# 1.3 FFN half-steps in every round of attention, with each weight unit's VectorE work behind the round's maximum

## The chip, the cores and the metric

The kernel runs on one core of a Trainium2 chip. The metric is the device time of one execution in microseconds (us). Three runs of the kernel before gave 940.33, 939.21 and 939.44 us, so the median is 939.44 us.

## What is computed

Three layers follow each other on 2304 tokens (4 batches of 576, 8 heads of 64, model width 512): linear attention with random features, a gated FFN (RMS norm, SiLU gate, hidden width 1536), and a mixture of 8 experts with capacity routing. Cut to what matters:

```
proj = x @ omega.T                 # per head: 64 -> 128 features, for q and for k
phi  = exp(h - max(h)) / sqrt(m)   # h = proj - |x|^2 / 2
kv, z = phi(k).T @ v, sum(phi(k)); attn = phi(q) @ kv / (phi(q) @ z + 1e-6)
xn   = attn / rms(attn) * rms_g    # 2304 x 512
y    = (silu(xn @ w_gate) * (xn @ w_val)) @ w_out
out  = top-capacity routing of y to 8 experts, each relu(y @ w1[e]) @ w2[e]
```

The weights `w_gate`, `w_val` and `w_out` come in as 64-bit floats and are turned into 32-bit ones on the chip.

## The kernel before

**Rounds of attention.** Attention is a list of 76 items: a `KItem` takes 256 or 128 key tokens of a head pair, a `QItem` half the heads of 128 query tokens. `run_tick(tick)`, called a *round* here, runs one lag of each of up to six items: lag 0 projects (TensorE, tile `pp`, L387 to L392), takes the maximum (VectorE, `mx`, L396) and the exponential (ScalarE, `ft`, L399); lag 1 is the product with v for keys (L439, L442) or the transposes for queries (L485); lag 2 the product with kv (L491, L496) and the division; lags 3 to 5 the norm and the transposes into the FFN's input blocks `xh`, `xl` (L501, L549, L550).

**Half-steps of the FFN.** An input block is 512 tokens (four of them, and a last one of 256). A *half-step* `(j, f, v)` is 12 matmuls of block `j`, 128 hidden columns `f`, gate (`v = 0`) or value (`v = 1`), into one PSUM tile `gv` (`ffn_pe`, L642 to L645). `gv` has two buffers (pool `psG`). `ffn_el` empties it: for the gate a tanh on ScalarE (L654) and a product on VectorE (L655), for the value a product on VectorE (L663 for block 0, L667 for the others). `ffn_step_pe` and `ffn_step_el` run the next half-step that is ready. There are 120 half-steps; the first block is ready at round 23, and the last rounds leave over 40 to a loop behind attention.

**Weight units.** The 36 units convert the 64-bit weights: 24 `WgvUnit` (gate and value, two for each `f`) and 12 `WoUnit`. A unit lives four lags: lag 0 a magnitude on ScalarE (L570), lag 1 `word()`, three VectorE operations (L574, L575, L576), lag 2 for a `WgvUnit` a cast on ScalarE (L598) and a difference on GpSimd (L599). A `WoUnit` has TensorE work too: at lag 2 four transposes into a `gv` tile (L613), emptied by ScalarE (L627), at lag 3 matmuls into the same tile (L617), emptied by two small VectorE operations into `wog` (L629, L630). So it holds one of the two `gv` buffers from its transposes until those. `conv_pe(pace)` adds `pace` to a due count and starts a unit for each whole one; `conv_el` runs the units' other operations and starts the load of a later one. Half-step `(0, f, v)` needs the two units of `f`.

**What sets the order.** TensorE's instructions stand in the order in which the code writes them. On the other engines a scheduler orders them at build time, by priority and by its own estimate of when each can run; attention's part has a raised priority. Every engine, and SP's queue of transfers, then runs its list strictly in that order. In a round the code writes: `conv_pe`, attention's TensorE part, a half-step, attention's other part, `conv_el`, loads, `ffn_step_el`. From round 23 on, as long as gate and value units are left, an extra pass adds one more unit and one more half-step (`SUB = 1`), so that such a round has two units and two half-steps; after that one half-step a round and half a unit. When a new input block needs a buffer that is taken (rounds 60 and 78), the rest of the old block is run off at once.

Of the kernel before, what the change touches and what calls it, by code (L numbers as in the profile page):

```python
# [14 lines left out]
OP = mybir.AluOpType  # L15
AX = mybir.AxisListType
# [18 lines left out]
KF = FF // 128  # L35
# [11 lines left out]
EARLY = 6  # L47
LOADS = 9
SKIP = 2
SUB = 1  # L50
PACE = (0.5, 1.0, 0.5)
FFN_AT = 23
AHEAD_A = 200
HB = 6
# [236 lines left out]
def kernel(ctx, tc, qT, kT, kC, v1, vC, om, wgv, rms, wo, wg2, w1, w2, cfd, trd, cid, out, dbg=None):  # L291
    nc = tc.nc
# [35 lines left out]
    st = {}  # L328
# [64 lines left out]

    def feat(pp, n, ng):
        mx = at.tile([128, 4], F32, name="mx")
        nc.vector.tensor_reduce(out=mx[:n, :ng], in_=pp[:n, :ng], axis=AX.X, op=OP.max, negate=True)  # L396
        ft = at.tile([128, 4, M], F32, name="ft")
        for g in range(ng):
            nc.scalar.activation(ft[:n, g], pp[:n, g], AF.Exp, bias=mx[:n, g:g + 1])  # L399
        return ft  # L400

    class KItem:
# [42 lines left out]
        def el(self, lag):  # L445
            b, p, g = self.b, self.p, self.g
            if lag == 0:
                self.ft = feat(self.pp, 128, 2 * len(self.ts))
            elif lag == 1 and g == 2:
                r, w = p // 2, b // 2  # L450
                if w not in kvs:
                    kvs[w] = at.tile([128, H, 2, D + 1], F32, name="kvs", bufs=1)
                nc.scalar.copy(kvs[w][:, 4 * r:4 * r + 4, b % 2, :].rearrange("p (o h) d -> p h o d", o=2),
                               st.pop(("pk", b, r))[:, :4 * (D + 1)].rearrange("p (h o d) -> p h o d", h=2, o=2))
# [123 lines left out]
    class WgvUnit(Unit):  # L578
# [9 lines left out]
        def el(self, lag):  # L588
            f, s_ = self.f, slice(self.g * 512, (self.g + 1) * 512)
            if lag == 0:  # L590
                self.magnitude(fp.tile([128, DM], F32, name="dw", bufs=DW))
            elif lag == 1:
                self.word()
            elif lag == 2:
                if self.g == 0:
                    wsl[f] = wpool.tile([128, 2, 1024], F32R, name="wc")
                w = wsl[f]
                nc.scalar.copy(w[:, 0, s_], self.t)  # L598
                nc.gpsimd.tensor_sub(w[:, 1, s_], self.t, w[:, 0, s_])  # L599
                gvs.add((f, self.g))  # L600

    class WoUnit(Unit):
# [16 lines left out]
        def el(self, lag):  # L619
            f = self.f  # L620
            if lag == 0:
                self.magnitude(fp.tile([128, DM], F32, name="dw", bufs=DW))
            elif lag == 1:
                self.word()
                nc.sync.dma_start(wo_dr[f], self.t)
            elif lag == 2:
                nc.scalar.copy(self.t, self.pt.rearrange("p k m -> p (k m)"))  # L627
            elif lag == 3:
                nc.vector.tensor_copy(wog[:, f, 0, :], self.pw)  # L629
                nc.vector.tensor_sub(wog[:, f, 1, :], self.pw, wog[:, f, 0, :])  # L630
                wogs.add(f)
# [16 lines left out]
    def ffn_el(j, f, v, pg):  # L648
        n = WIDTH[j]
        nh = n // HB2  # L650
        if v == 0:
            fst["th"] = fp.tile([128, BLK], F32, name="th")
            th = fst["th"][:, :n]
            nc.scalar.activation(th, pg, AF.Tanh, scale=0.5)  # L654
            nc.vector.scalar_tensor_tensor(th, th, 1.0, pg, op0=OP.add, op1=OP.mult)  # L655
            return
        th = fst["th"][:, :n]
        hp = fp.tile([128, BLK // HB2, 2, HB2], F32R, name="hp")
        hf = hp.bitcast(F32)
        dst = h_dr[nh * j:nh * j + nh] if nh > 1 else h_dr[NT // HB2 - 1:]  # L660
        dst = dst[:, :, f].rearrange("b p x -> p b x")
        if j == 0:
            nc.vector.scalar_tensor_tensor(hf[:, :, 0], pg.rearrange("p (b t) -> p b t", b=nh), 0.5,  # L663
                                           th.rearrange("p (b t) -> p b t", b=nh), op0=OP.mult, op1=OP.mult)
            nc.sync.dma_start(dst[:, :, :HB2], hf[:, :, 0])
            return
        nc.vector.scalar_tensor_tensor(th, pg, 0.5, th, op0=OP.mult, op1=OP.mult)  # L667
        h = th.rearrange("p (b t) -> p b t", b=nh)
        nc.scalar.copy(hp[:, :nh, 0], h)  # L669
        nc.gpsimd.tensor_sub(hp[:, :nh, 1], h, hp[:, :nh, 0])  # L670
        nc.sync.dma_start(dst, hf[:, :nh].rearrange("p b l t -> p b (l t)"))
        fq.append((j, f, hp))
# [30 lines left out]
    def ffn_rank_el():  # L703
        for c0 in rks:
            ranks(nc, st["eng"], fp, cf[:, C_T:C_N].rearrange("p (a b) -> p a b", b=E), L, R, c0, 2)
        rks.clear()

    def ffn_step_pe():
        if not ready or ready[0][1:] not in gvs or (fq and fq[0][1] not in wogs):
            return False  # L710
        j, f, v = ready.pop(0)
        pg = ffn_pe(j, f, v)
        if (f, v) == (KF - 1, 1):
            del xblk[j]
        ffn_rank()
        if v and fq:
            ffn_lg(*fq.pop(0))
        fst["el"] = (j, f, v, pg)
        return True

    def ffn_step_el():
        if "el" in fst:
            j, f, v, pg = fst.pop("el")
            ffn_el(j, f, v, pg)
            ffn_rank_el()
            return j, f, v
        return None
# [43 lines left out]
            nc.tensor.matmul(sink, idle[:, :128], idle[:, 128:], start=True, stop=True)  # L771

    NLAG = 6
    conv = dict(live=[], due=0.0, next=0, load=3)

    def conv_pe(pace):
        conv["due"] += pace
        conv["live"] = [(lag + 1, u) for lag, u in conv["live"] if lag < 3]
        while conv["due"] >= 1 and conv["next"] < len(useq):
            conv["due"] -= 1  # L780
            conv["live"].append((0, useq[conv["next"]]))
            conv["next"] += 1
        for lag, u in conv["live"]:
            u.pe(lag)

    def conv_el():
        for lag, u in conv["live"]:
            u.el(lag)
            if lag == 1 and conv["load"] < len(useq):
                useq[conv["load"]].load()  # L790
                conv["load"] += 1

    def run_tick(tick):
        live = [(lag, items[tick - lag]) for lag in range(NLAG) if 0 <= tick - lag < len(items)]
        conv_pe(PACE[0] if tick < FFN_AT else PACE[1] if conv["next"] < 2 * KF else PACE[2])
        with tc.high_priority(offset=AHEAD_A):
            for lag, it in live:
                it.pe(lag)
        ffn_step_pe()
        for lag, it in live:  # L800
            if lag == 5 and isinstance(it, QItem) and it.hf and it.c * 128 // BLK not in xblk:
                while len(xblk) > 1:
                    ffn_step_el()
                    if not ffn_step_pe():
                        conv_el()
                        conv_pe(1)
        with tc.high_priority(offset=AHEAD_A):
            for lag, it in live:
                it.el(lag)
            if tick + 1 < len(items):  # L810
                items[tick + 1].split()
        conv_el()
        if tick + AHEAD < len(items):
            items[tick + AHEAD].load()
        ffn_step_el()
        if tick >= FFN_AT and conv["next"] < 2 * KF:
            for r in range(SUB):
                conv_pe(1)
                ffn_step_pe()
                conv_el()  # L820
                ffn_step_el()

    with tc.manual_schedule(engines={mybir.EngineType.PE}):
        warm(10)
        for tick in range(len(items) + NLAG - 1):
            run_tick(tick)
            if tick < 2:
                warm(4)
# [41 lines left out]
    lates, step = [], 0  # L870
# [327 lines left out]
```

## Time and profile before

| | us |
|---|---|
| median of three runs | 939.44 |
| the profiled execution's own time | 941.22 |
| its span (first to last instruction) | 939.4 |
| TensorE busy in the span | 912.3 (97%) |
| VectorE, ScalarE, GpSimd busy | 536.6, 372.5, 220.8 |

The profiled execution took 1.8 us more than the median; 1.8 us of its own time lies around the span. The trace has, for each instruction, its engine, line, tile, start and duration, and for idle time what ended it. TensorE's matmuls overlap, so that a matmul's duration is longer than the distance to the next; time is therefore best read from one start to another. "PEclk" is the clock that TensorE was granted, as a share of 2.4 GHz.

### The profile page before, as it was taken

What the parts mean: (1) busy time and instruction counts of PE and PEld (TensorE: products, weight loads), DVE (VectorE), ACT (ScalarE), POOL (GpSimd) and SP (SyncE); (2) the same over time, 40 slices, a digit from 0 to 9 for tenths busy, and PEclk for the clock granted to TensorE, in tenths of its full rate; (3) what the DMA queues carried; (4) which work ended last, traced back from release to release, by engine and by line L of the source; (5) the groups of instructions that cost most, each with busy time, mean ns of one, the idle gap of its engine ahead of it and who ended that gap; (6) DMA issues with size and microseconds to landing.
All of it is one profiled execution on the core that took longest, in us unless ns stands there. A gap on an engine that the chain in (4) does not pass through costs nothing.

```text
span 939.4 us, 16221 instructions
## 1 busy us (share of the span) xinstructions
PE 912.3 (97%) x6219; PEld 792.0 (84%) x6219; DVE 536.6 (57%) x1230; ACT 372.5 (40%) x843; POOL 220.8 (24%) x294
## 2 busy tenths in 40 slices
PE   8998889999999999999999999999999999999996
PEld 7887679888888888777789777777779999999996
DVE  3799976655542455341255566666664655566651
ACT  5975445554553445233233110010014444455441
POOL 1345421122232332254323000000011222121211
PEclk9998989999999999999999999999999999999998
DMA  8546653354222121158665477767632666666650
GB/s 289 178 155 211 212 169 117 124 189 163 68 71 92 61 90 46 70 211 288 205 202 201 148 210 210 207 198 211 183 93 90 181 202 192 201 194 187 186 170 26
DMA packets 111486, 152.61 MB, mean 162 GB/s; under 512 B 6448, under 2 KB 70576, under 8 KB 111408
## 3 DMA queue, kind: packets, MB, share of 16 engines
q1 hardware_dynamic: 105600, 137.28, 46.8%
q0 software_dynamic: 3072, 9.44, 3.3%
q10 hardware_dynamic: 2736, 4.85, 1.4%
q8 instruction: 49, 0.80, 0.4%
q14 instruction: 29, 0.24, 0.1%
HBM read 107.50 MB, written 44.04 MB: 161 GB/s over the span
## 4 chain that ended last, share of the span: by engine, by line
PE 75%; issue 6%; DVE 2%; POOL 2%; DMA 1%; ACT 0%; SPq 0%; POOLq 0%; ACTq 0%; DVEq 0%
PE py L953 15%; PE gv L642 9%; PE gv L643 9%; PE gv L645 9%; PE ph L1067 3%; PE ph L1064 3%; PE ph L1065 3%; PE py L1075 3%; PE py L1076 3%; PE py L1077 3%; PE pm L496 2%; PE cnt L180 2%; PE pm L439 1%; PE pp L387 1%; PE pm L485 1%
## 5 line engine op out<-in xcount | busy, mean ns | idle before, releaser
L642 PE MATMUL gv<-xh,wc 128*128 128x512 f32 (+1 forms) x480 | 182.1, 386 | 8.0 <-DVE th L655 8.0
L643 PE MATMUL gv<-xh,wc 128*128 128x512 f32 (+1 forms) x480 | 176.4, 374 | 0.0
L953 PE MATMUL py<-wc,ht 128*128 128x512 f32 x648 | 167.3, 404 | 0.0
L953 PEld LDWEIGHTS py<-wc,ht 128*128 128x128 f32 x648 | 114.8, 189 | 19.0
L645 PE MATMUL gv<-xl,wc 128*128 128x512 f32 (+1 forms) x480 | 120.0, 372 | 0.0
L642 PEld LDWEIGHTS gv<-xh,wc 128*128 128x128 f32 x480 | 91.9, 191 | 27.5 <-DVE th L655 9.4
L643 PEld LDWEIGHTS gv<-xh,wc 128*128 128x128 f32 x480 | 91.9, 191 | 14.4
L645 PEld LDWEIGHTS gv<-xl,wc 128*128 128x128 f32 x480 | 86.5, 191 | 16.1
L655 DVE SCALAR_TENSOR_TENSOR th<-th,gv 128x512 f32<-128x512 f32 (+1 forms) x60 | 37.9, 631 | 103.8 <-ACT th L654 103.7
L399 ACT ACTIVATE ft<-pp,mx 128x128 f32<-128x128 f32 x288 | 82.8, 373 | 26.1 <-DVE mx L396 23.4
L924 DVE TENSOR_TENSOR wc<-ws,wc 128x512 fp32r<-128x512 f32 x128 | 84.7, 682 | 0.0
L670 POOL TENSOR_TENSOR hp<-th,hp 128x512 fp32r<-128x512 f32 (+1 forms) x48 | 58.7, 1222 | 107.5 <-ACT hp L669 101.5
L1075 PE MATMUL py<-ehh,wc 128*128 128x288 f32 x256 | 77.7, 304 | 0.0
L1076 PE MATMUL py<-ehl,wc 128*128 128x288 f32 x256 | 75.9, 297 | 0.0
L1077 PE MATMUL py<-ehh,wc 128*128 128x288 f32 x256 | 75.8, 296 | 0.0
L1064 PE MATMUL ph<-exh,wc 128*128 128x288 f32 x256 | 71.6, 302 | 0.0
L1065 PE MATMUL ph<-exh,wc 128*128 128x288 f32 x256 | 69.8, 295 | 0.0
L934 ACT CAST wc<-ws 128x1024 fp32r<-128x1024 f32 x64 | 66.9, 1046 | 2.4 <-ACT ys L964 2.4
L964 ACT COPY ys<-py 128x512 f32<-128x512 f32 x18 | 10.6, 588 | 144.2 <-PE py L953 103.3
L654 ACT ACTIVATE th<-gv 128x512 f32<-128x512 f32 (+1 forms) x60 | 33.2, 554 | 65.5 <-PE gv L645 60.0
L396 DVE TENSOR_REDUCE mx<-pp 128x4 f32<-128x512 f32 (+1 forms) x76 | 49.8, 656 | 15.9 <-PE pp L392 8.4
L669 ACT CAST hp<-th 128x512 fp32r<-128x512 f32 (+1 forms) x48 | 27.1, 565 | 77.7 <-DVE th L667 77.6
(217 smaller groups left out, 1709.7 us busy)
## 6 DMA issues: line engine op xcount, KB each, us to landing
ws<-in_w_dram SPq DMA_DIRECT2D x64, 512.0 KB, 4.4
ht<-h_dr SPq DMA_DIRECT2D x54, 512.0 KB, 4.2
h_dr<-hp SPq DMA_DIRECT2D x36, 512.0 KB, 2.8
ws<-in_wgv_dram SPq DMA_DIRECT2D x24, 512.0 KB, 4.1
h_dr<-hp SPq DMA_DIRECT2D x24, 256.0 KB, 2.3
ws<-in_wo_dram SPq DMA_DIRECT2D x12, 512.0 KB, 3.8
h_dr<-ht SPq DMA_DIRECT2D x12, 512.0 KB, 3.6
y_dr<-ys ACTq DMA_DIRECT2D x18, 256.0 KB, 4.3
```

What stands on the lines that cost most here:

```text
L399: nc.scalar.activation(ft[:n, g], pp[:n, g], AF.Exp, bias=mx[:n, g:g + 1])
L642: nc.tensor.matmul(pg[:, :n], w[:, 0, v, k], xh[:, k, :n], start=(k == 0), stop=False)
L643: nc.tensor.matmul(pg[:, :n], w[:, 1, v, k], xh[:, k, :n], start=False, stop=False)
L645: nc.tensor.matmul(pg[:, :n], w[:, 0, v, k], xl[:, k, :n], start=False, stop=(k == KD - 1))
L924: nc.vector.tensor_sub(w[:, 1, h], sv[:, h], w[:, 0, h])
L934: nc.scalar.copy(w[:, 0], sv)
L953: nc.tensor.matmul(py, ht[:, i4, a], w[:, l, f % 2], start=(f == 0 and n == 0), stop=(f == KF - 1 and n == 2))
L1064: nc.tensor.matmul(ph, w[:, 0, k, m], xh[:, k], start=(k == 0), stop=False)
L1065: nc.tensor.matmul(ph, w[:, 1, k, m], xh[:, k], start=False, stop=False)
L1075: nc.tensor.matmul(py, w[:, 0, k], hh[:, k], start=(k == 0), stop=False)
L1076: nc.tensor.matmul(py, w[:, 0, k], hl[:, k], start=False, stop=False)
L1077: nc.tensor.matmul(py, w[:, 1, k], hh[:, k], start=False, stop=(k == KE - 1))
```

## The change

The extra pass goes. In its place every round from 23 on adds 0.3 to a count, and a second half-step is run whenever that count reaches one: 1.3 half-steps a round to the end of attention. The units' pace becomes 0.5, 0.9 and 0.7 a round: ahead of round 23, while gate and value units are left, and for the `WoUnit`s. A unit's `word()` is wrapped so that its VectorE operations stand behind the maximum of the same round in VectorE's list. And `ffn_step_el` is written ahead of `conv_el`.

```diff
-SUB = 1
-PACE = (0.5, 1.0, 0.5)
+STEP = 1.3
+PACE = (0.5, 0.9, 0.7)
@@ feat
-        nc.vector.tensor_reduce(out=mx[:n, :ng], in_=pp[:n, :ng], axis=AX.X, op=OP.max, negate=True)
+        st["mx"] = nc.vector.tensor_reduce(out=mx[:n, :ng], in_=pp[:n, :ng], axis=AX.X, op=OP.max, negate=True)
@@ WgvUnit.el and WoUnit.el
             elif lag == 1:
-                self.word()
+                with tc.issue_after(st["mx"].ins):
+                    self.word()
@@ run_tick
+        ffn_step_el()
         conv_el()
         if tick + AHEAD < len(items):
             items[tick + AHEAD].load()
-        ffn_step_el()
-        if tick >= FFN_AT and conv["next"] < 2 * KF:
-            for r in range(SUB):
-                conv_pe(1)
+        if tick >= FFN_AT:
+            conv["step"] += STEP - 1
+            if conv["step"] >= 1:
+                conv["step"] -= 1
                 ffn_step_pe()
-                conv_el()
                 ffn_step_el()
```

**VectorE, rounds 24 and 25.** A list of the kernel before, from one round's maximum to the next (the numbers behind the names tell tiles apart; `dw` is a unit's word, `th` and `hp` are the half-steps' results, `kh` a query tile's cast):

```order
L396 TENSOR_REDUCE mx_882<-pp_857 128x4
L576 SCALAR_TENSOR_TENSOR dw_683<-ws_472,dw_683 128x512
L574 TENSOR_SCALAR dw_757<-dw_757 128x512
L575 SCALAR_TENSOR_TENSOR dw_757<-ws_554,dw_757 128x512
L576 SCALAR_TENSOR_TENSOR dw_757<-ws_554,dw_757 128x512
L574 TENSOR_SCALAR dw_829<-dw_829 128x512
L655 SCALAR_TENSOR_TENSOR th_906<-th_906,gv_869 128x512
L575 SCALAR_TENSOR_TENSOR dw_829<-ws_645,dw_829 128x512
L576 SCALAR_TENSOR_TENSOR dw_829<-ws_645,dw_829 128x512
L663 SCALAR_TENSOR_TENSOR hp_932<-gv_909,th_906 128x2x256
L574 TENSOR_SCALAR dw_852<-dw_852 128x512
L396 TENSOR_REDUCE mx_959<-pp_935 128x4
```

The changed kernel's list from the maximum of round 27 to that of round 29 (line numbers are up to two higher there):

```order
L396 TENSOR_REDUCE mx_1018<-pp_997 128x2
L382 CAST kh_1069<-qt_931 128x256
L657 SCALAR_TENSOR_TENSOR th_994<-th_994,gv_981 128x512
L574 TENSOR_SCALAR dw_979<-dw_979 128x512
L575 SCALAR_TENSOR_TENSOR dw_979<-ws_876,dw_979 128x512
L576 SCALAR_TENSOR_TENSOR dw_979<-ws_876,dw_979 128x512
L665 SCALAR_TENSOR_TENSOR hp_1027<-gv_1005,th_994 128x2x256
L396 TENSOR_REDUCE mx_1061<-pp_1039 128x4
L382 CAST kh_1115<-qt_1037 128x256
L657 SCALAR_TENSOR_TENSOR th_1073<-th_1073,gv_1048 128x512
L396 TENSOR_REDUCE mx_1106<-pp_1081 128x4
```

Between two maxima there were eight word operations and two half-steps' results, with word operations on both sides of `th`; now there are three and two in one round and none and one in the next, and `th` stands ahead of the words.

**TensorE, a `WoUnit` and the half-steps beside it.** Before, around the second unit (`gv_1541` is the unit's tile, the other `gv` tiles are half-steps):

```order
L645 MATMUL gv_1497<-xl_548,wc_1070 128x512 x4
L613 MATMUL gv_1541<-cf_69,dw_1471 128x128 x4
...
L485 MATMUL pm_1553<-cf_69,ft_1512 128x128 x4
L496 MATMUL pm_1558<-kvs_256,qp_1517 128x65 x4
L501 MATMUL pm_1563<-cf_69,xn_1461 128x128 x4
...
L645 MATMUL gv_1568<-xl_548,wc_1070 128x512 x4
L617 MATMUL gv_1541<-wg2s_81,dw_1471 128x8 x4
```

The changed kernel, around its fifth unit (`gv_2224`) and the start of its sixth (`gv_2300`):

```order
L614 MATMUL gv_2224<-cf_69,dw_2164 128x128 x4
...
L439 MATMUL pm_2124<-vt_2037,ft_2200 128x65 x4
...
L647 MATMUL gv_2240<-xl_1482,wc_370 128x512 x4
L683 MATMUL lg_2142<-hp_2156,wog_74 16x512
L684 MATMUL lg_2142<-hp_2156,wog_74 16x512
...
L647 MATMUL gv_2280<-xl_1482,wc_501 128x512 x4
L618 MATMUL gv_2224<-wg2s_81,dw_2164 128x8 x4
L614 MATMUL gv_2300<-cf_69,dw_2220 128x128 x4
```

Before, one half-step lay between a unit's two TensorE parts, and attention's part between any two uses of a `gv` buffer. Now a second half-step (`gv_2280`) can lie there with only the two `lg` matmuls ahead of it, and the next unit's transposes can follow a unit's matmuls at once.

**ScalarE, ahead of round 23.** Before, the cast of round 23's keys (`kh_779`) stood ahead of round 21's exponentials (`ft_745`):

```order
L549 CAST xh_547<-pm_700 128x4x128
L364 CAST kh_779<-kt_728 128x256
L399 ACTIVATE ft_745<-pp_732,mx_743 128x128 x4
L364 CAST kh_822<-kt_728 128x256
L570 ACTIVATE dw_504<-ws_351 128x512
L399 ACTIVATE ft_774<-pp_759,mx_772 128x128 x2
```

Now:

```order
L549 CAST xh_547<-pm_700 128x4x128
L399 ACTIVATE ft_745<-pp_732,mx_743 128x128 x2
L399 ACTIVATE ft_774<-pp_759,mx_772 128x128
L399 ACTIVATE ft_745<-pp_732,mx_743 128x128
L399 ACTIVATE ft_774<-pp_759,mx_772 128x128
L364 CAST kh_779<-kt_728 128x256
L364 CAST kh_822<-kt_728 128x256
```

The two casts moved behind the exponentials of rounds 21 and 22, and one magnitude (`dw_504`) ahead of them.

## Rows read from the trace of the kernel before

**Rows 1.** The page: busy time of each engine, share of the span, instructions.

```profile
PE 912.3 (97%) x6219; PEld 792.0 (84%) x6219; DVE 536.6 (57%) x1230; ACT 372.5 (40%) x843; POOL 220.8 (24%) x294
```

**Rows 2.** Windows: stretch, length, busy PE, PEld, DVE, ACT, POOL, PEclk, DMA share, GB/s.

```profile
80.00:100.00 20.00, 16.63 (x76) 13.86 (x76) 19.75 (x25) 9.77 (x21) 10.72 (x8) 0.83 0.66 206
100.00:120.00 20.00, 16.05 (x84) 13.05 (x83) 19.45 (x27) 11.43 (x25) 9.69 (x8) 1.00 0.70 205
120.00:140.00 20.00, 16.68 (x86) 13.90 (x85) 14.64 (x41) 7.69 (x21) 3.82 (x6) 0.83 0.50 168
160.00:180.00 20.00, 20.00 (x143) 18.34 (x141) 13.46 (x31) 10.63 (x28) 3.38 (x6) 1.00 0.40 128
```

**Rows 3.** Waits of TensorE in 60 to 140 us: total, times, longest.

```profile
PE gv L642 <- DVE th L655: 7.1, 5, 3.4
PE pm L485 <- ACT ft L399: 2.4, 2, 2.1
PE pm L491 <- DVE x L518: 1.5, 1, 1.5
```

**Rows 4.** TensorE's timeline, rounds 23 to 26: start, us, operation, idle before.

```profile
59.01 0.50 PE L642 MATMUL gv<-xh,wc 128*128 128x512 f32 x1
64.59 0.28 PE L387 MATMUL pp<-omh,kh 128*128 128x256 f32 x1
71.75 0.28 PE L387 MATMUL pp<-omh,kh 128*128 128x256 f32 x1
...
84.43 0.79 PE L642 MATMUL gv<-xh,wc 128*128 128x512 f32 x1 [3.37 <-DVE th L655]
89.72 0.48 PE L642 MATMUL gv<-xh,wc 128*128 128x512 f32 x1
```

**Rows 5.** VectorE operations of 0 to 420 us by shape: busy us, mean ns.

```profile
L396 DVE TENSOR_REDUCE mx<-pp 128x4 f32<-128x512 f32 x68 | 46.5, 684 | 11.6 <-PE pp L392 7.5 <-PE pp L389 2.1 <-ACT wc L598 1.0
L575 DVE SCALAR_TENSOR_TENSOR dw<-ws,dw 128x512 int32<-128x512 int32 x36 | 34.0, 948 | 0.8 <-DVE dn L514 0.3
L576 DVE SCALAR_TENSOR_TENSOR dw<-ws,dw 128x512 int32<-128x512 int32 x36 | 28.8, 803 | 0.5
L655 DVE SCALAR_TENSOR_TENSOR th<-th,gv 128x512 f32<-128x512 f32 x38 | 26.0, 684 | 58.6 <-ACT th L654 58.6
L574 DVE TENSOR_SCALAR dw<-dw 128x512 int32<-128x512 int32 x36 | 23.2, 646 | 4.4 <-ACT dw L570 4.4
```

**Rows 6.** TensorE's timeline, a later round of queries without a wait.

```profile
143.62 0.37 PE L387 MATMUL pp<-omh,kh 128*128 128x256 f32 x1
146.06 0.48 PE L642 MATMUL gv<-xh,wc 128*128 128x512 f32 x1
```

**Rows 7.** Timelines of two engines: what follows a unit's matmuls and a gate's half-step.

```profile
137.48 1.05 PE L617 MATMUL gv<-wg2s,dw 128*128 128x8 f32 x8
138.39 0.36 PE L387 MATMUL pp<-omh,kh 128*128 128x256 f32 x1
...
138.64 0.17 DVE L629 CAST wog<-gv 128x8 fp32r<-128x8 f32 x1 [0.23 <-PE gv L617]
...
295.78 1.07 PE L645 MATMUL gv<-xl,wc 128*128 128x512 f32 x4
296.68 0.39 PE L642 MATMUL gv<-xh,wc 128*128 128x512 f32 x1
297.58 0.69 DVE L655 SCALAR_TENSOR_TENSOR th<-th,gv 128x512 f32<-128x512 f32 x1 [3.17 <-ACT th L654]
```

**Rows 8.** A window of 5 us, columns as in rows 2.

```profile
110.00:115.00 5.00, 3.10 (x17) 2.46 (x15) 4.93 (x6) 1.81 (x4) 3.00 (x3) 1.00 0.57 176
```

**Rows 9.** ScalarE and GpSimd operations on key tiles, 0 to 420 us, as in rows 5.

```profile
L364 ACT CAST kh<-kt 128x256 fp32r<-128x256 f32 x24 | 10.0, 417 | 3.8 <-PE pp L388 3.7
L365 POOL TENSOR_TENSOR kl<-kt,kh 128x256 fp32r<-128x256 f32 x24 | 18.0, 749 | 53.8 <-ACT kh L364 38.2 <-PE pm L485 6.9 <-PE pm L442 4.8
L570 ACT ACTIVATE dw<-ws 128x512 f32<-128x512 f32 x36 | 24.4, 678 | 33.7 <-issue 24.4 <-DMA ws<-in_wgv_dram 9.1 <-DMA ws<-in_wo_dram 0.2
```

More of the change, by code (lines that the diff above doesn't have):

```diff
@@ L623, in el @@
             elif lag == 1:
-                self.word()
+                with tc.issue_after(st["mx"].ins):
+                    self.word()
                 nc.sync.dma_start(wo_dr[f], self.t)
@@ L773 @@
     NLAG = 6
-    conv = dict(live=[], due=0.0, next=0, load=3)
+    conv = dict(live=[], due=0.0, next=0, load=3, step=0.0)
     def conv_pe(pace):
```

## The prediction

> **What bounds the kernel now.** I read the busy shares first, then windows of 20 us, then the waits inside the windows that stand out, then the timelines of the engines named there. TensorE is busy for 912.3 of 939.4 us [rows 1], so nearly all that an order can win is in its 27 us of idle time and in time at a lower clock. The windows show where that lies: from 80 to 140 us TensorE is busy for 16 to 17 of each 20 us while VectorE is busy for 19.75 and 19.45, and in two of the three the granted clock averages 0.83 of the full 2.4 GHz, so a part of them ran at 1.2 [rows 2]. From 160 us on TensorE is busy all the time and VectorE two thirds of it. So there is one stretch bound by VectorE, in a kernel that is otherwise bound by TensorE.
>
> The waits of 60 to 140 us name the mechanism: TensorE waited 7.1 us in five places for the operation that empties a gate's half-step, 2.4 us for exponentials, 1.5 us for a division [rows 3], 11.0 us together. That VectorE operation was late because word operations stood ahead of it in VectorE's list. The longest wait shows the second loss: the half-step behind it takes 84.43 to 89.72, 5.29 us, where two undisturbed ones take 59.01 to 64.59, 2.79 us each [rows 4]: 2.50 us more, at the lower clock.
>
> What the stretch loses: 11.0 us of waits; and by the clock at most 2 x 20 us x (1 - 0.83) = 6.8 us [rows 2]. The first of these two 3.4 us cost 2.50 us in matmuls; taken for both that is 5.0. I take the middle, 5.9. Together **16.9 us**, between 16.0 and 17.8.
>
> **The change part by part.**
>
> *Fewer units and half-steps a round.* A word costs 0.646 + 0.948 + 0.803 = 2.40 us of VectorE, a half-step's product or a maximum 0.684 us [rows 5]. Before, VectorE's list has 16 words, 12 products, six maxima (one of them half as long) and four smaller operations of 2 us in rounds 23 to 28: 51.8 us. TensorE needs 71.75 - 64.59 = 7.16 us for such a round with two half-steps [rows 4], 43.0 us for six. VectorE has 8.8 us too much to do, and that is what the waits are made of. In the changed lists rounds 23 to 36 have 17 words, 18 products and 14 maxima, and with casts, divisions and norms VectorE's sum by the same means is 75.1 us. TensorE needs 18 half-steps of 2.79, six attention parts of 7.16 - 5.58 = 1.58, and eight of queries at up to 146.06 - 143.62 = 2.44 us [rows 6]: 79.2 us. VectorE is no longer over, but level. TensorE's own work is the same, instruction for instruction, so the 16.9 us go in full, less what is lost anew.
>
> *What is lost anew on VectorE.* Single rounds are still over: round 26 has 2 words and 3 single operations more, some 8.1 us against 7.16, round 27 about 0.7 us over. The half-step behind a round's maximum covers most of this. In the new lists the products stand ahead of the words, and words are five or more units ahead of the half-steps that need them, so nobody waits for a word itself. Nothing lost is one bound; three such pairs lost in full, 5 us, the other. I take 1.0, nearer the first, because the sums leave 4 us of room.
>
> *The word behind the maximum.* What is queued behind the maximum is then the word, and behind it products and the next round's maximum. A word that waits costs nothing by itself; what it could delay is a `WoUnit`'s transposes one round later, a half-step (2.79 us) after the maximum, against 2.40 for the word. I cost it at nothing; the cover is that half-step, and without it the price is some 0.3 us a unit.
>
> *The buffers of `gv`.* This is new. A `WoUnit` holds one of two buffers from its transposes to its last VectorE operation. At a pace of 0.7 with 1.3 half-steps, the changed TensorE list has three places where the next unit's transposes follow a unit's matmuls into the same buffer, three more where they take the buffer of the half-step just run, and two where a half-step follows a half-step into the only free buffer. Before there were none: attention's part always lay between. Prices [rows 7]: after a unit's last matmul TensorE could go on at 138.39; the first of two VectorE operations starts at 138.64 and takes 0.17, so with a second like it and 0.1 for the signal (as from 138.53 to 138.64) 139.08, a wait of 0.69. After a gate's half-step TensorE could go on at 296.68; its product ends at 298.27, with the signal 298.37, a wait of 1.69. After a value's there is no tanh: 0.17 + 0.1 + 0.68 + 0.1 less two `lg` matmuls of 0.23, 0.6. In the other three a unit's matmuls (138.39 - 137.48 = 0.91) and mostly two `lg` matmuls cover that. Sum: 3 x 0.69 + 0.6 + 1.69 = **4.4 us**; bounds 1.5 (only the gate's is left) and 8, where VectorE or ScalarE reaches five of these 0.7 us later.
>
> The Trainium skill ("Perfetto Trace Analysis", section Matmuls) says that independent matmul groups should rotate through PSUM banks so that emptying one overlaps the next group; the eight places break this rule. By the row, the overlap lost differs by place and sums to 4.4 us; by the rule, taken to expose each emptying in full, an estimate is three times that, which is a rival below.
>
> *Rounds 0 to 22.* Round 23's keys are now cast behind round 22's exponentials: cast 0.42 and difference 0.75 [rows 9] then lie on TensorE's path, while two casts fewer (0.83) and one magnitude more (0.68) lie ahead of those exponentials. I take +0.5, between -1 and +2.
>
> *Transfers.* SP's list has the same transfers; unit loads still wait for a free stage behind the word that frees it. A round now starts fewer units, so each load has more time. Nothing. Behind round 40, and in the loop after attention, TensorE is never idle before [rows 2], and gets the same work: the run-off of round 60 is spread, which wins nothing.
>
> **Sum.** -16.9 + 1.0 + 4.4 + 0.5 = -11.0 us. Against the profiled execution's own 941.2 us that is 930.2; that execution stood 1.8 above the median, and against the median of 939.44 it is **928.4 us**.
>
> **The rivals.**
>
> *Clean.* The new waits vanish in slack and nothing is lost on VectorE: 939.4 - 16.9 = 922.5. For it: the products now stand early. Against: the two half-steps into one buffer have nothing else to run.
>
> *The buffers cost in full.* Each of the eight places exposes a whole emptying of 1.69: 13.5 + 1.5 - 16.9 = -1.9, 937.5. For it: a list that is level has no room to be early. Against: a unit's emptying has no tanh in it. This is what the skill's rule above would give.
>
> *The clock falls at every new wait* (the other side). Mechanism: short waits of TensorE between half-steps, five at the `gv` buffers and two in rounds 23 to 40, each followed by a half-step at 1.2 GHz for 2.50 us more: 17.5 + 5.9 - 16.9 = +6.5, 945.9. It decides from the fifth slow half-step on. For it: the two low stretches before follow waits. Against: from 110 to 115 us TensorE was idle for 1.9 of 5 us at full clock [rows 8]. The Trainium skill ("TensorE: Matmul & The Clock Gate", section A second HAM failure mode: psum-queue depth-cycling) tells of exactly such a swing from short idles between groups. The row of 110 to 115 us does not agree, those of 80 to 100 us could.
>
> *It doesn't do what it says.* If a half-step finds its weights or `wog` unready when the code is written out, it is skipped, and the loop behind attention has to run it: about 939. The changed list has 67 half-steps ahead of round 75 where there were 62, so this is nearly excluded.
>
> **How the numbers follow.** Forecast (924.5 to 933.5) 0.57; clean 0.21; buffers in full 0.13; clock 0.05; not done 0.04. A measurement of this kernel tells some 0.2%, 1.9 us, from no change: faster is below 937.6, slower above 941.3. Of the buffer rival a little less than half lies within. Faster: 0.57 + 0.21 + 0.08 = 0.86; same: 0.05 + 0.04 = 0.09; slower 0.05. The range goes from just under the clean case, with 1 us won in the first rounds, to where the buffers cost 8 us and VectorE 5: 921.5 to 936. It leaves out the clock rival, the undone case, the upper half of the buffer rival, and a little below.
>
> **What would show it.** Right: from 80 to 140 us TensorE is busy for over 19 of each 20 us at a clock of 1.00, and VectorE for some 17 or 18. The wait of `gv` on L655's successor falls from 7.1 us to 2 or 3, and new waits of 0.5 to 1.7 us stand before the `WoUnit` transposes and before two half-steps, some 4 us between 165 and 265 us. From there on nothing changes but that everything comes about 11 us earlier. Wrong: the clock under 1.00 in 165 to 265 us (the clock rival); waits there of over 8 us (the buffers); or waits for exponentials or keys beyond 3 us in 30 to 100 us, which would mean that the words behind the maximum, or the moved casts, push attention's own chain.

## The result, and the profile after

The changed kernel takes 928.82 us (median of four runs, 928.50 to 929.55); the kernel before, on the same chip, took 939.47. The ratio is 0.9886 (95% interval 0.9869 to 0.9903): 10.65 us faster, where 11.0 us were forecast. The profiled execution took 928.50 us with a span of 926.7. The two profiled spans differ by more, 12.7 us: the section on why comes back to this.

The page's busy line, which answers to [rows 1]:

```profile
PE 905.5 (98%) x6219; PEld 786.7 (85%) x6219; DVE 526.7 (57%) x1226; ACT 373.4 (40%) x843; POOL 226.1 (24%) x298
```

The same windows as [rows 2], with the one ahead of them (columns as there):

```profile
60.00:80.00 20.00, 17.07 (x100) 14.60 (x99) 18.19 (x26) 12.21 (x31) 11.88 (x10) 1.00 0.67 213
80.00:100.00 20.00, 19.69 (x108) 16.66 (x108) 17.02 (x33) 11.57 (x29) 8.64 (x8) 1.00 0.61 179
100.00:120.00 20.00, 19.73 (x123) 17.11 (x122) 18.42 (x42) 12.35 (x32) 9.09 (x10) 1.00 0.51 144
120.00:140.00 20.00, 20.00 (x118) 17.55 (x117) 18.36 (x34) 14.24 (x35) 9.53 (x12) 1.00 0.52 160
160.00:180.00 20.00, 19.38 (x123) 17.27 (x124) 11.11 (x19) 8.94 (x23) 3.70 (x4) 1.00 0.43 138
```

From 80 to 140 us TensorE is busy all but 0.3 us of each 20, at full clock, with VectorE at 17.0 to 18.4. One poor stretch is left, 60 to 80 us, which was the good one before:

```profile
60.00:80.00 20.00, 19.67 (x103) 16.73 (x103) 19.73 (x26) 11.96 (x29) 10.78 (x9) 1.00 0.70 213
```

The waits of TensorE in 60 to 140 us (total, times, longest), beside [rows 3], and below them those of 140 to 270 us, where there were none before:

```profile
PE gv L644 <- DVE th L657: 2.9, 2, 2.7
PE pm L485 <- ACT ft L399: 0.3, 1, 0.3
PE gv L644 <- DVE hp L665: 0.3, 1, 0.3
...
PE gv L614 <- DVE wog L632: 1.8, 3, 0.6
PE gv L644 <- DVE th L657: 1.4, 1, 1.4
PE gv L644 <- DVE th L669: 0.3, 1, 0.3
PE gv L614 <- DVE dw L576: 0.2, 1, 0.2
```

The first group fell from 11.0 to 3.5 us; the waits for exponentials and for the division are as good as gone. The second is new, 3.7 us. Nearly all of the 3.5 is one wait, in round 26. Here it is on TensorE (the end of that round's first half-step, and its second), and below it what VectorE and GpSimd did meanwhile:

```profile
72.49 1.07 PE L647 MATMUL gv<-xl,wc 128*128 128x512 f32 x4
76.22 0.50 PE L644 MATMUL gv<-xh,wc 128*128 128x512 f32 x1 [2.66 <-DVE th L657]
...
70.36 0.67 DVE L576 SCALAR_TENSOR_TENSOR dw<-ws,dw 128x512 int32<-128x512 int32 x1
70.96 1.51 DVE L574 TENSOR_SCALAR dw<-dw 128x512 int32<-128x512 int32 x1
72.50 1.67 DVE L575 SCALAR_TENSOR_TENSOR dw<-ws,dw 128x512 int32<-128x512 int32 x1
74.09 0.68 DVE L396 TENSOR_REDUCE mx<-pp 128x4 f32<-128x512 f32 x1
75.50 0.67 DVE L657 SCALAR_TENSOR_TENSOR th<-th,gv 128x512 f32<-128x512 f32 x1
...
70.40 3.23 POOL L600 TENSOR_TENSOR wc<-dw,wc 128x512 fp32r<-128x512 f32 x2 [3.25 <-ACT wc L599]
```

The result that TensorE waits for (75.50) stands behind the maximum of round 26 (74.09), and that behind words that took 1.51 and 1.67 us instead of 0.42 and 0.69. Both ran beside GpSimd's differences of other units (70.40 to 73.63), and the 2.07 us more that they took are most of the 2.66.

Two of the places at the `gv` buffers, a unit's matmuls with the next unit's transposes, and a half-step behind a gate's half-step:

```profile
158.43 0.95 PE L618 MATMUL gv<-wg2s,dw 128*128 128x8 f32 x8
159.93 0.63 PE L614 MATMUL gv<-cf,dw 128*128 128x128 f32 x4 [0.55 <-DVE wog L632]
...
261.59 1.07 PE L647 MATMUL gv<-xl,wc 128*128 128x512 f32 x4
264.06 0.50 PE L644 MATMUL gv<-xh,wc 128*128 128x512 f32 x1 [1.41 <-DVE th L657]
266.02 1.08 PE L647 MATMUL gv<-xl,wc 128*128 128x512 f32 x4
266.94 0.40 PE L683 MATMUL lg<-hp,wog 128*16 128x512 f32 x1
```

From 158.43 to 159.93 are 1.50 us. A unit's matmuls that nobody follows into the same buffer take 0.81 to the next start (267.41 to 268.22), so this place costs 0.69 us, and the wait shown, 0.55, is a little less than what is lost, since a matmul's end is modelled. The gate's costs (264.06 - 261.59) - (266.94 - 266.02) = 1.55 us.

### The profile page after: what moved, and what is told of

Its sections match the earlier page's. It is cut to its first block, busy times and chain, and to the rows that moved or that the text cites. A ratio compares the mean times of both kernels' runs of the same rounds, so it can differ in the third digit from the quotient of the medians.

```text
span 926.7 us, 16209 instructions
## 1 busy us (share of the span) xinstructions
PE 905.5 (98%) x6219; PEld 786.7 (85%) x6219; DVE 526.7 (57%) x1226; ACT 373.4 (40%) x843; POOL 226.1 (24%) x298
## 4 chain that ended last, share of the span: by engine, by line
PE 71%; issue 6%; DVE 2%; POOL 2%; DMA 1%; ACT 0%; POOLq 0%; DVEq 0%; ACTq 0%
PE py L955 16%; PE gv L644 8%; PE gv L645 8%; PE gv L647 8%; PE ph L1069 3%; PE ph L1066 3%; PE ph L1067 3%; PE py L1077 3%; PE py L1078 3%; PE py L1079 3%; PE cnt L180 2%; PE pm L496 1%; PE pm L439 1%; PE lg L684 1%; PE gv L618 1%
## 5 line engine op out<-in xcount | busy, mean ns | idle before, releaser
L644 PE MATMUL gv<-xh,wc 128*128 128x512 f32 (+1 forms) x480 | 180.3, 382 | 5.3 <-DVE th L657 4.7
L645 PE MATMUL gv<-xh,wc 128*128 128x512 f32 (+1 forms) x480 | 174.4, 370 | 0.0
L644 PEld LDWEIGHTS gv<-xh,wc 128*128 128x128 f32 x480 | 90.6, 189 | 23.2 <-DVE th L657 6.3
L645 PEld LDWEIGHTS gv<-xh,wc 128*128 128x128 f32 x480 | 90.6, 189 | 13.7
L647 PEld LDWEIGHTS gv<-xl,wc 128*128 128x128 f32 x480 | 85.3, 189 | 15.7
L1071 DVE SCALAR_TENSOR_TENSOR ehl<-ph,ehh 128x288 fp32r<-128x288 f32 x64 | 29.3, 458 | 46.8 <-ACT ehh L1070 46.8
```

The source lines that it names most:

```text
L644: nc.tensor.matmul(pg[:, :n], w[:, 0, v, k], xh[:, k, :n], start=(k == 0), stop=False)
L645: nc.tensor.matmul(pg[:, :n], w[:, 1, v, k], xh[:, k, :n], start=False, stop=False)
L647: nc.tensor.matmul(pg[:, :n], w[:, 0, v, k], xl[:, k, :n], start=False, stop=(k == KD - 1))
```

## The experiments

How the parts act on VectorE's list is seen from the number of word operations between one round's maximum and the next, counted in the lists as they are written out (the names are those of the runs below):

```
round                        23 24 25 26 27 28 29 30 31 32 33 34
before                        7  8  8  8  7  9  5  3  3  1  3  0
e1  word alone                6  9  8  8  7  6  3  3  3  0  3  0
the change                    5  3  5  7  3  0  3  3  3  3  3  3
e2  without the word          4  5  5  7  4  6  7  3  4  5  4  4
e3  two units a round         5  3  5  7  4  5  8 16  3  0  3  3
e10 half-steps as before      6  8  3  3  3  0  3  3  3  2  4  2
e8  slower until round 26     5  3  5  4  0  3  3  3  3  3  3  3
e11 one unit a round          3  3  3  3  3  3  3  3  3  3  3  3
```

**e1: the word behind the maximum alone.**

```diff
 # before, and only:
+                with tc.issue_after(st["mx"].ins):
+                    self.word()
```

> The kernel before with only the word behind the maximum of its round; TensorE's list is that of before. Theory 'sums' (the gain comes from VectorE having fewer words and products per TensorE time): rounds 23 to 28 still hold about 15 words and 12 products, 8.8 us more than TensorE needs, so 937.5 to 941, and the wait of gv on th in 60 to 140 us stays at 6 us or more. Rival 'word' (where a word stands in the list is what counts): 928 to 932, wait under 3 us.

Measured 940.74 us, ratio 1.0013 (0.9999 to 1.0026): no gain. TensorE still waits 6.4 us for `th`, and 4.0 us in one place for a word:

```profile
PE gv L644 <- DVE th L657: 6.4, 5, 2.9
PE gv L614 <- DVE dw L576: 4.0, 1, 4.0
```

As theory "sums" said: 44 of 47 word operations still lie in rounds 23 to 28. By itself this part only moves the losses. The waits for exponentials and for the division, 3.9 us before, are gone; instead `WoUnit` transposes wait for their words, 4.0 us here and 2.2 us in 140 to 270 us, where before had no wait.

**e2: the change without it.**

```diff
-                with tc.issue_after(st["mx"].ins):
-                    self.word()
+                self.word()
```

> The changed kernel without the word behind the maximum; TensorE's list is that of the change. Theory 'sums': 928 to 931, since VectorE's work per TensorE time is that of the change; words that move ahead of products may cost 1 or 2 us. Rival 'word': 936 to 940, the wait of gv on th back at 6 us or more.

Measured 935.32 us, ratio 0.9948 (0.9929 to 0.9967). Neither theory: against the kernel before in the same set (939.73) 4.4 us are won, so some 6 of the 10.65 are lost. The waits show where:

```profile
PE gv L642 <- DVE th L655: 3.3, 3, 1.7
PE pm L485 <- ACT ft L399: 1.6, 1, 1.6
PE pm L491 <- DVE x L518: 1.5, 1, 1.5
PE pm L496 <- DVE x L518: 0.5, 1, 0.5
```

The waits for exponentials and for the division are back at 1.6 and 2.0 us, and those for `th` are 3.3. Rounds 27 to 34 hold 37 word operations where the change has 21: left to itself, the scheduler draws words forward and stacks them ahead of attention's operations. So the pace spreads the words only in part (31 operations in rounds 23 to 28, where before has 47 and the change 23) unless something holds them in their round.

**e3: two units a round.**

```diff
-PACE = (0.5, 0.9, 0.7)
+PACE = (0.5, 2.0, 0.7)
```

> The changed kernel with two gate and value units a round (2.0 in place of 0.9), half-steps still at 1.3. Theory 'sums': rounds 26 to 31 then have some 15 words (36 us), 7 products and 6 maxima (9 us) and 5 us of smaller operations, 50 us against some 31 of TensorE: 10 to 19 us lost, 938 to 948, in waits for exponentials, divisions and th, with a lower clock in that stretch. Rival (the rate of half-steps or the order of the list made the gain): 928 to 932.

Measured 952.34 us, ratio 1.0131 (1.0110 to 1.0152), 23.5 us more than the change; the forecast of the sums, 938 to 948, was too low. One wait makes most of it; below it the window in which it ends:

```profile
PE gv L614 <- DVE dw L576: 15.0, 1, 15.0
```

```profile
100.00:120.00 20.00, 4.99 (x27) 4.17 (x26) 16.85 (x30) 8.98 (x18) 9.54 (x7) 0.72 0.59 183
```

In round 30 sixteen word operations stand between two maxima, and a `WoUnit`'s transposes wait 15.0 us for one of them, with a granted clock of 0.72. All waits of 60 to 140 us are 21.4 us. That VectorE's list sets the time there is borne out, and the price was higher than the 19 us of excess that the sums gave. But the place was another than expected: not exponentials or divisions, and `th` only for 4.7 us, but a unit's transposes that wait for the unit's own word, behind all words that stand ahead of it.

**e4 and e10: the half-steps as before.** In e4 two half-steps a round run as long as gate and value units are left, which at the slower pace lasts longer than it did before; e10 keeps to rounds 23 to 28.

The condition in e4:

```diff
-            conv["step"] += STEP - 1
-            if conv["step"] >= 1:
-                conv["step"] -= 1
+            if conv["next"] < 2 * KF:
```

and in e10:

```diff
-            conv["step"] += STEP - 1
-            if conv["step"] >= 1:
-                conv["step"] -= 1
+            if tick < FFN_AT + 6:
```

> The changed kernel with half-steps as before: two a round while gate and value units are left, then one; units at 0.9 and 0.7. Theory 'sums': 0.9 word, two products and a maximum are 4.7 us a round against 7.16, so VectorE is not over, and there are fewer double half-steps among the WoUnits: 925 to 930. Rival (1.3 half-steps a round made the gain): the waits of th return with two half-steps a round, 934 to 940.

> The changed kernel with the half-steps as they were before: two a round in rounds 23 to 28, one from 29 on, so that the first block lasts until the second is ready; units at 0.9 and 0.7 a round. Theory 'units' (the spread of the units, with the word behind the maximum, makes the gain): rounds 23 to 28 hold 23 word operations where they held 47, VectorE is not over, 926 to 931. Theory 'half-steps' (the even rate of half-steps makes it): 935 to 940, because rounds with one half-step are short against VectorE's list. Between the two: each has a share.

e4 took 939.75 us, ratio 0.9995 (0.9983 to 1.0008), as the rival said, but not by the rival's waits: `th` is at 2.6 us. The half-steps ran ahead of their weights and then of the input block:

```profile
PE gv L644 <- ACT wc L599: 1.7, 1, 1.7
PE gv L645 <- POOL wc L600: 0.9, 1, 0.9
...
PE gv L618 <- ACT dw L629: 2.3, 1, 2.3
```

TensorE waits for a unit's cast and difference, and two rounds (36 and 40) have no half-step at all; the wait for a unit's copy comes straight behind round 40. So e4 mixed two things. e10, which doesn't, took 932.14 us, ratio 0.9918 (0.9901 to 0.9934): between the theories. Against before in the same set it wins 7.6 us, so of the 10.65 us some 3 go with the even rate of half-steps and the rest with the spread of the units with the word held in its round. The 3 us are not certain: the two intervals just touch, and of the 4.0 us between the two profiled spans 2.4 lie ahead of round 23, where VectorE and ScalarE run the same lists in both. Nor do they lie in the stretch of 60 to 140 us, where e10 waits for 2.1 us and the change for 3.5; e10 has 5.1 us of waits in 140 to 270 us, where the change has 3.7, and one of 1.0 behind that.

**e5: the order of the half-step's second part.**

```diff
-        ffn_step_el()
         conv_el()
...
+        ffn_step_el()
```

> The changed kernel with the half-step's second part again behind the units' operations and loads. TensorE's list is that of the change, VectorE's differs in a few places. Theory (this part is worth nothing): 928 to 930. Rival (it is what brings the half-steps' results ahead of the words): 931 to 936, with 3 us or more of additional waits on th in 60 to 140 us.

Measured 931.30 us, ratio 0.9912 (0.9896 to 0.9928), against 0.9886 and, in another set, 0.9887 (0.9868 to 0.9905) for the change: the intervals overlap. In the profile the same wait, 2.9 us, falls on another operation. What this part is worth lies between nothing and some 2.5 us, and stays open.

**e7 and e8: the buffers, and the units left over.** In e7 a `WoUnit`'s transposes come behind attention's TensorE part, so that attention lies between a unit's matmuls and the next transposes, and no second half-step runs in a round in which a unit takes a buffer. e8 also starts the faster pace four rounds later. e7:

```diff
@@ conv_pe
-            u.pe(lag)
+            if lag != 2:
+                u.pe(lag)
+
+    def conv_turn():
+        for lag, u in conv["live"]:
+            if lag == 2:
+                u.pe(lag)
@@ run_tick
+        conv_turn()
         ffn_step_pe()
...
-            if conv["step"] >= 1:
+            if conv["step"] >= 1 and not any(lag == 2 and isinstance(u, WoUnit) for lag, u in conv["live"]):
```

e8, in addition:

```diff
-PACE = (0.5, 0.9, 0.7)
+PACE = (0.5, 1.0, 0.7)
-        conv_pe(PACE[0] if tick < FFN_AT else ...
+        conv_pe(PACE[0] if tick < FFN_AT + 4 else ...
```

> The changed kernel with a WoUnit's transposes behind attention's TensorE part, not ahead of it, and a second half-step put off while a WoUnit holds a buffer. Theory (the 3.7 us of waits in 140 to 270 us come from gv buffers with nothing in between): these waits go to under 1 us, 924.5 to 926.5. Rival (ScalarE's copy of the transposes is then late for the unit's matmuls, one half-step behind them): a new wait of that copy, 928 or more.

> As the run with the transposes behind attention, and the units' pace stays at 0.5 until round 26, then 1.0: rounds 23 to 26 have 18 word operations where they had 20, and round 26 four where it had seven. Theory (the 2.7 us wait of round 26 is the words still left over from the rounds ahead): that wait falls under 1 us, 922 to 925. Rival (it is the late load or ScalarE): the wait stays, the same time as that run.

e7 took 924.05 us, ratio 0.9831 (0.9814 to 0.9847), some 5 us better than the change. In 140 to 270 us no wait is left, and the windows that had them are full:

```profile
160.00:180.00 20.00, 20.00 (x130) 18.02 (x130) 12.11 (x22) 9.77 (x24) 4.41 (x5) 1.00 0.45 145
180.00:200.00 20.00, 20.00 (x126) 17.41 (x125) 12.97 (x22) 9.31 (x25) 4.85 (x5) 1.00 0.58 196
```

ScalarE's copy is not late for the matmuls. e8 took 923.48 us, ratio 0.9833 (0.9815 to 0.9850), the same within the intervals, and the wait of round 26 is still 2.7 us: the words that it takes away (four in place of seven) stand behind the result that TensorE waits for, those of rounds 23 to 25 ahead of it. This edit missed the cause.

**e11: one unit a round from round 23 on.** On top of e7 the pace ahead of round 23 is so low that nothing is left over.

```diff
-PACE = (0.5, 0.9, 0.7)
+PACE = (0.35, 1.0, 0.7)
```

> As the run with the transposes behind attention, with units at 0.35 a round ahead of round 23 and 1.0 from there: the list then has three word operations a round (one unit) from round 23 on, where it had 5, 3, 5 and 7, and th stands straight behind the maximum. Theory (the 2.7 us wait of round 26 is VectorE with the units left over from the rounds ahead): no wait over 1 us in 60 to 140 us, no low clock there, 920 to 922.5. Rival (the scheduled list isn't what holds th, but ScalarE or a transfer): the wait stays, 923 to 925.

Measured 923.45 us (920.66 to 924.21), ratio 0.9819 (0.9801 to 0.9837); the profiled execution, at 920.66, is the fastest of all. The wait is gone, and the window of 60 to 80 us is full:

```profile
PE gv L644 <- DVE th L657: 0.2, 1, 0.2
```

```profile
60.00:80.00 20.00, 20.00 (x115) 17.45 (x114) 16.15 (x24) 11.05 (x27) 10.05 (x10) 1.00 0.63 186
```

So the 2.7 us came from words that were left over from the rounds ahead; their number and the time that they took beside GpSimd fell together, and this edit doesn't tell the two apart. The time forecast for this, 920 to 922.5, was missed: the median is not told from e7's and e8's by its interval. The profile has 1.0 us of new waits for keys ahead of round 23, which eats some of it, and round 23 starts at 56.81 instead of 55.37. e7, e8 and e11 all beat both kernels.

**e13: a unit's difference on VectorE.** On e11.

```diff
-                nc.gpsimd.tensor_sub(w[:, 1, s_], self.t, w[:, 0, s_])
+                nc.vector.tensor_sub(w[:, 1, s_], self.t, w[:, 0, s_])
```

> As that run, with a unit's difference on VectorE in place of GpSimd. Theory (word operations are stretched, from 0.68 to as much as 1.67 us, while GpSimd works on SBUF): the means of the two two-input word operations fall from 0.87 and 0.73 us to 0.7 each, and the difference takes some 0.7 us of VectorE, so VectorE's sum stays within 5 us and the time within 2 us. Rival (the stretch has another cause, such as transfers): the means stay at 0.8 us or more.

One run, 922.66 us. VectorE's rows (busy us, mean ns) of e11, then of e13:

```profile
L575 DVE SCALAR_TENSOR_TENSOR dw<-ws,dw 128x512 int32<-128x512 int32 x36 | 31.7, 880 | 0.7
L576 DVE SCALAR_TENSOR_TENSOR dw<-ws,dw 128x512 int32<-128x512 int32 x36 | 25.2, 699 | 0.7
L574 DVE TENSOR_SCALAR dw<-dw 128x512 int32<-128x512 int32 x36 | 21.7, 603 | 0.0
```

```profile
L575 DVE SCALAR_TENSOR_TENSOR dw<-ws,dw 128x512 int32<-128x512 int32 x36 | 29.0, 806 | 0.8
L576 DVE SCALAR_TENSOR_TENSOR dw<-ws,dw 128x512 int32<-128x512 int32 x36 | 25.2, 701 | 0.7
L574 DVE TENSOR_SCALAR dw<-dw 128x512 int32<-128x512 int32 x36 | 17.8, 494 | 0.0
L600 DVE TENSOR_TENSOR wc<-dw,wc 128x512 fp32r<-128x512 f32 x24 | 17.5, 734 | 1.9 <-ACT wc L599 1.6
```

The time stays, as forecast. The means fall by 0.07, 0.00 and 0.11 us. Of the two that were to reach 0.7, L576 was there already in e11, and L575 stays at 0.81, which by its mean alone is the rival's sign. GpSimd keeps the differences of keys, queries and half-steps: 11 of the 36 L575 operations still run beside one of its operations and take 1.07 us in the mean, the other 25 take 0.68 to 0.69. What the two engines' timelines say of each instruction is in the last section.

**e14 and e15: the change and the kernel before again,** unchanged, for second profiles.

> The change itself once more, for a second profile and beside these versions on one chip: 928.5 to 930. If the low clock follows a wait by chance and not by rule, a stretch of it may appear in 76 to 90 us, as in two other versions with the same 2.7 us wait, for 1.7 us at most.

> The kernel before once more, for a second profile: 939 to 941; the same waits of 11 us in 60 to 140 us. If the 1.8 us by which the first profiled execution stood above the median was the low clock of 10 to 20 us, an execution near the median has none there and three or four stretches in 60 to 150 us.

The change took 929.42 us (928.56 to 931.08) beside a median of 940.20 for the kernel before, ratio 0.9887 (0.9868 to 0.9905): the same gain, 10.8 us. The kernel before had one execution of 938.42 us with a span of 936.6. Its windows and waits of 60 to 140 us:

```profile
0.00:20.00 20.00, 18.37 (x90) 15.38 (x91) 8.55 (x18) 11.36 (x32) 3.34 (x7) 1.00 0.90 318
80.00:100.00 20.00, 16.20 (x73) 13.46 (x74) 19.83 (x26) 9.36 (x19) 9.79 (x8) 0.91 0.63 185
120.00:140.00 20.00, 17.02 (x98) 14.77 (x97) 15.06 (x42) 8.17 (x22) 3.50 (x5) 0.91 0.52 171
```

```profile
PE gv L642 <- DVE th L655: 8.3, 6, 3.4
PE pm L485 <- ACT ft L399: 2.4, 2, 2.1
PE pm L491 <- DVE x L518: 1.5, 1, 1.5
```

The waits are the ones that were known, 12.2 us here. The clock isn't: it is at 1.00 in the first 20 us, where the first profile had 0.83 in 10 to 20 us, and at 0.91 in two windows where that had 0.83. The change's second execution has 0.92 in 60 to 80 us and 0.99 in 80 to 100, where its first has 1.00.

## Why the prediction was right, and which steps were not

The sum was right by its size, -11.0 against -10.65 and -10.8. That it came so close is in part luck, as the terms show. With two profiles of each kernel they can be held against what was measured:

| term | predicted | first profiles | second profiles |
|---|---|---|---|
| waits of 60 to 140 us of before, gone | -11.0 | -11.0 | -12.2 |
| waits left there | +1.0 | +3.5 | +3.2 |
| low clock in 60 to 140 us | -5.9 | -5.9 (estimate) | about -2 |
| waits at `gv` in 140 to 270 us | +4.4 | +3.7 | +3.7 |
| start of round 23 | +0.5 | -1.9 | +0.8 |
| a wait behind attention | none | -0.9 | -2.0 |
| sum | -11.0 | -12.5 | -8.5 |
| spans | | -12.7 | -9.0 |

The -5.9 of the first pair is the prediction's own estimate for the two windows at 0.83; the change has 1.00 there. "About -2" are two windows at 0.91, 2 x 20 x 0.09 = 3.6 us at most, less 20 x 0.08 + 20 x 0.01 = 1.8 in the change. The first pair's extra 1.9 us ahead of round 23 is largely the start of before's profiled execution: at 0.83 over 10 us it loses up to 1.7, about what it stood above the median. The forecast was made against the median, so this didn't enter it. Against the forecast went the waits left, 2.2 to 2.5 us more, and in the second pair the clock, some 4 us less; for it a wait behind attention that went without having a term (0.9 to 2.0) and 0.7 us less at `gv`. They cancel in part.

**Right: what bound the stretch, and that it would go.** VectorE's list was over by 8.8 us in rounds 23 to 28, and the waits that this made are gone, with TensorE busy from 80 us on and VectorE at 17.0 to 18.4, where 17 or 18 were named. (The "17 words" of rounds 23 to 36 are 47 operations, 15.7 words; the sum of 75.1 us fits these.) e3, which has two units a round, brings back 21.4 us of waits there.

**Right: the buffers of `gv`.** The three unit-after-unit places cost 0.69, 0.76 and 0.76 us from start to start, where 0.69 was worked out; the gate's place 1.55 for 1.69; the value's 0.49 (195.39 - 194.67, less the usual 0.23; 0.33 by the wait shown) for 0.6; the three covered places show no wait. That is some 4.2 us from start to start, for 4.4. The 0.18 us that is left of the waits shown is a unit's transposes waiting for the unit's word, not for a buffer. e7, which takes all of them away, is some 5 us better (924.05 against 928.82 and 929.42). The Trainium skill's rule ("Perfetto Trace Analysis", section Matmuls) that groups should rotate through PSUM banks so that emptying one overlaps the next group held in its direction: e7 has the same two buffers, but attention's work between two uses of one. Its full price, 13.5 us, did not come: three of the eight places show no wait at all, and four of the other five cost less than 0.8 us.

**Wrong in size: "I take 1.0, nearer the first, because the sums leave 4 us of room".** 3.5 us were left, inside the bounds of nothing to 5. The sum was taken over rounds 23 to 36, while the excess sits in rounds 23 to 26, which hold 20 word operations, among them units left over from before round 23. By the prediction's own means these four rounds need 21.7 us of VectorE and 20.3 of TensorE (five half-steps, four attention parts), some 1.5 too much. The durations in the trace sum to 23.6: the 20 word operations took 17.9 us and not 16.0, because many ran beside GpSimd (last section). e11, with three a round, has 0.2 us left. The room of later rounds can't be used by an earlier one.

**Wrong: "A word that waits costs nothing by itself ... I cost it at nothing".** The price of delay was indeed next to nothing in the change, 0.18 us in one place (in e1 it was 6.2 us), but the part's worth wasn't: e2 loses some 6 us without it. The sums were counted in the list with all parts in it, so they were right while the reading of which part made them was not. And e1 shows that it has no worth with the old pace. So the parts' worths don't add up to the 10.65.

**Wrong in size: the clock's 5.9 us.** That was one execution's. Another of the same kernel lost at most 3.6. The prediction took the dips of one profile for a property of the list.

**Missed: "Behind round 40, and in the loop after attention, TensorE is never idle before".** The trace of before has a wait of 0.9 us for `th` at 415.71, and its second profile one of 2.0 at 413.15. The five profiles with 62 half-steps ahead of round 75 (before twice, e1, e4, e10) all have one of 0.9 to 2.7 us in 270 to 420 us; none of the nine with 67 has. Why the number matters was not tried.

**Rounds 0 to 22** can't be told: the wait for the first exponentials alone took 1.85 and 0.20 us in two executions of before and 0.59 and 1.55 in two of the change.

**The rivals.** "Clean" fell by the 3.5 and the 3.7 us. "Buffers in full" fell by the places' own prices. "The clock falls at every new wait" fell too: none of the waits at `gv` was followed by a window under 1.00. The wait of round 26 was followed by one in some executions (below), for at most 1.8 us (0.09 of 20, in e5). That the change doesn't do what it says was excluded by the 67 half-steps.

## What to carry to other kernels

Where an in-order engine's list is over in one stretch, compare its sum with the bound engine's round by round and not over the stretch: leftovers of the rounds ahead count in full. Spreading work by a pace is worth less if a scheduler is free to draw it forward (without the dependence 4.4 of 10.65 us were left here); hold it in its round with a dependence, and judge the two edits together. Two uses of one buffer should have another engine phase between them: with attention's part there, some 5 us went.

## What the runs showed of the hardware

**VectorE's word operations are stretched while GpSimd works.** In the change's timelines of 0 to 300 us, L575 took 0.67 to 0.69 us in the 14 cases with GpSimd idle, and 0.68 to 1.67, 1.04 in the mean, in the 22 beside a GpSimd operation; L574 took 0.41 to 0.43 and up to 1.51. Maxima and half-steps' results, which read PSUM, took the same either way (the results 0.67 to 0.69). In e13 no word operation without GpSimd beside it took more than 0.69, and with it up to 1.67. Transfers, the rival of e13, are not the cause: with GpSimd idle, L576 took 0.68 us at 29.24 us of the change's profile, where transfers moved some 410 GB/s. The Trainium skill ("GPSIMD Engine Reference", section 1. Specifications) says that GpSimd's SBUF interfaces are shared with VectorE, with contention for instructions that have two SBUF inputs or run in a 2-port mode; the trace agrees for L575 and L576, which read two SBUF tensors. L574 reads one; in which mode it runs no run here shows. So the 2.40 us of a word that the prediction summed with is a mean over both: 0.42 + 0.69 + 0.69 = 1.80 with GpSimd idle.

**The same wait is not always followed by a low clock.** The change twice, e5, e7 and e8 have nearly the same list up to round 26 and a wait of 2.6 to 2.9 us in it. The windows of 60 to 100 us in the change's second execution:

```profile
60.00:80.00 20.00, 17.10 (x89) 14.30 (x88) 18.24 (x25) 12.24 (x32) 12.25 (x10) 0.92 0.69 208
80.00:100.00 20.00, 20.00 (x113) 17.39 (x112) 16.39 (x32) 11.70 (x29) 8.62 (x8) 0.99 0.65 186
```

The clock was under 1.00 there in three of the five (0.91 in e5, 0.92 in the change's second execution, 0.94 in e7) and 1.00 in two. Its cost was small: round 27 came 81.06 - 79.08 = 1.98 us later than in the first execution, of which 0.37 were there at round 23, and at round 30 the difference was 1.03 (95.60 against 94.57). The 0.95 us in between were made up in round 29: its transposes need exponentials that came only 0.33 us later than in the first execution (88.08 against 87.75), and the first execution waited for them there while the second did not. The Trainium skill ("TensorE: Matmul & The Clock Gate", section A second HAM failure mode: psum-queue depth-cycling) tells of a clock that swings with short idles between matmul groups; the idles at the `gv` buffers, 0.2 to 1.4 us, show none of it here.
